# Spacing the router's counts, the token transposes and the weight conversions between the matmuls of a fused attention and expert kernel

## The chip, the cores and the metric

The kernel is one program on one core of a Trainium2 chip. The metric is the device time of one launch in microseconds (us), the median of the runs shown. The kernel before took 1327.54 us, the median of 3 runs (1324.36, 1327.54 and 1327.96). A profile of one execution comes with it.

## The reference, cut to what matters

Three stages follow each other. Block-diagonal attention (8 batches, 8 heads, 576 positions in chunks of 64, head size 64) gives 4608 tokens of 512 numbers. A greedy router then gives every token to one of 8 experts, 576 tokens each, and each expert is a two-layer network. A dense network over all tokens ends it.

```python
logits = x @ w_gate                     # 4608 x 8
for idx in argsort(-logits.flatten()):  # greedy: best pair first
    tok, e = idx // E, idx % E
    if assigned[tok] >= 0 or counts[e] >= cap: continue
    assigned[tok] = e; counts[e] += 1
out[mask_e] = relu(x[mask_e] @ w1[e]) @ w2[e]        # 512 -> 1024 -> 512, per expert
y = max(out @ m1, out @ m2, out @ m3) @ m_out        # 512 -> 768 -> 512, relu inside
```

Matrix products of the experts and of the dense network are run as three products of split numbers (high times high, low weight times high, high weight times low), which is why each weight chunk and each activation has a "hi" and a "lo" tile.

## The kernel before, in words

After attention the kernel knows the logits (tile `L`). The routing is done in 8 rounds, one per expert that fills up. Round 0 runs alone; rounds 1 to 7 are woven between the matmuls of the experts. The order of all instructions is written out by hand: each engine runs its own instructions in the order in which the program issues them.

The weaving works by **places**. The expert loop calls `pump()` after every 6 matmuls of 288 columns, 64 times for each expert (32 times in the first layer, line L777, and 32 in the second, L806), so there are 512 places. `pump()` takes one step of three Python generators: `assign` (the routing), `prepare` (gathering and transposing the tokens of the next expert) and `convert` (rewriting the dense network's weights from 64 bit to 32 bit); at every second place it also calls `pump_loads()`, which splits one landed weight chunk into hi and lo (`split`, L577 on ScalarE, L578 on VectorE) if one is old enough, and issues one new 512 KB load on the SP queue. A `yield n` in a generator means: nothing more of this for n places. If the tokens of the next expert are not all transposed when its turn comes, `pump()` is called without matmuls.

`Router.round` is one round. Rounds 1 to 6 hold 5 search steps that narrow down a threshold. One step is: compare the bids with 32 levels (`ge`, L411, two VectorE instructions); 4 places later a first count on TensorE (L425, 9 matmuls), and VectorE takes from it the products that are wanted (`cs`, L428); one place later a second count (L433, 4 matmuls) and two short VectorE instructions (`fl`, `fb`); one place later a last small matmul (L441) and the new lower bound (`lo`, L443), with which the next step starts at the same place. Around the steps a round has a start (L353 to L399, then 5 places), the selection (L449 to L473), the positions (L478 to L491), the list of token numbers (L497, L504), and the bookkeeping (L509 to L519): in all 50 places. Round 7 has no search step. The chosen expert's 8 weight chunks can be asked for from the selection on (`expert`).

`prepare` gathers the 576 tokens (L597), waits 14 places (10 in round 1), and then transposes one 128-token tile at each place, five in all (`x_tr`: 4 TensorE transposes into one of two PSUM tiles `pxt` at L620, a ScalarE copy `xhi` at L622, a VectorE subtraction `xlo` at L623). It starts no sooner than the first layer of the expert before is through, since `xhi` and `xlo` have one buffer each.

`convert` works through 48 pieces of the dense weights; each is a load of 256 KB (tile `c64`, two buffers, L658), 7 VectorE instructions (L668 to L689), one at each step, and a store (L690). Before round 7 is done it takes a step at every second place, after that at every place. Loads and stores are both on the SP queue. Chunks of the dense weights are asked for only when their pieces are converted.

After expert 7 the dense network runs over 9 blocks of 512 tokens (L857, L880). In block 0 `pump()` and one more step of `convert` follow every 3 matmuls, so that what is left of the conversion runs there at two steps per 3 matmuls. `yload` (L734) brings the block's activations, 1 MB, and `ysplit` (L745, L746) splits them; block 1's load uses the same buffer as block 0's. The first layer's two PSUM tiles `acc` are freed by ScalarE's `ta` (L864) and VectorE's `tb` (L866).

Of the kernel before, what the change touches and what calls it, by code (L numbers as in the profile page):

```python
# [270 lines left out]
class Router:  # L271
# [111 lines left out]
    def round(s, r, PS, e_ready):  # L383
# [18 lines left out]
        for i in range(0 if last else NSTEP):  # L402
            mark("r.step")
            if i:
                lev = W.tile([128, J], F32, name="lev")
                nc.vector.tensor_scalar(lev, s.jw[:, i], lo, None, op0=OP.add)
            else:
                lev = s.lev0
            ge = W.tile([128, G, J], BF, name="ge")
            for a, b in ((0, 18), (18, G)) if r else ((0, 16), (16, 28), (28, G)):  # L410
                nc.vector.tensor_tensor(ge[:, a:b], bid[:, a:b, None].to_broadcast([128, b - a, J]),  # L411
                                        lev[:, None, :].to_broadcast([128, b - a, J]), op=OP.is_ge)
            if r + i == 0:
                s.begin2()
            if r == 0:
                mark("r.cnt")
                pc = PS.tile([128, E], F32, name="rp", tag="rp", bufs=2)
                for c in range(G):
                    nc.tensor.matmul(pc[:J, :], ge[:, c, :], oh[:, c, :], start=c == 0, stop=c == G - 1)  # L419
            else:  # L420
                yield 4
                mark("r.cnt")
                pk = PS.tile([128, 4, E], F32, name="rp", tag="rp", bufs=2)
                for c in range(0, G, 4):
                    nc.tensor.matmul(pk.rearrange("p c e -> p (c e)"), ge[:, c:c + 4].rearrange("p c j -> p (c j)"),  # L425
                                     oh[:, c:c + 4].rearrange("p c e -> p (c e)"), start=c == 0, stop=c == G - 4)
                cs = W.tile([128, 4, E], F16, name="cs")
                nc.vector.tensor_tensor(cs, pk, s.same, op=OP.mult)  # L428
                yield 1
                mark("r.cnt2")  # L430
                pc = PS.tile([128, E], F32, name="rp", tag="rp", bufs=2)
                for c in range(4):
                    nc.tensor.matmul(pc[:J, :], s.lev1, cs[:, c], start=c == 0, stop=c == 3)  # L433
            fl = W.tile([128, 1], F32, name="fl")
            fb = W.tile([128, 1], BF, name="fb")
            nc.vector.tensor_reduce(fl[:J], pc[:J], op=OP.max, axis=AX.X)
            nc.vector.tensor_scalar(fb[:J], fl[:J], CAP - .5, None, op0=OP.is_ge)
            yield 1
            mark("r.lo")
            pn = PS.tile([128, 1], F32, name="rp", tag="rp", bufs=2)  # L440
            nc.tensor.matmul(pn, s.ones[:J, :], fb[:J], start=True, stop=True)  # L441
            nlo = W.tile([128, 1], F32, name="lo", bufs=2)
            nc.vector.scalar_tensor_tensor(nlo, pn, s.ws[:, i:i + 1], lo, op0=OP.mult, op1=OP.add)  # L443
            lo = nlo
# [79 lines left out]
def kernel(ctx, tc, q, k, v, w_gate, w1, w2, m1, m2, m3, m_out, out, mark=lambda n: None):  # L524
# [18 lines left out]
    state = {"issued": 0, "used": 0, "w1": -1, "idx": -1, "pump": 0, "conv": 0}  # L543
# [37 lines left out]
    def pump_loads():  # L581
        for x in inflight:
            x[1] += 1
        if inflight and inflight[0][1] > 6:
            split()
        issue()
# [4 lines left out]
    def gather(r):  # L591
        mark("gather")
        xg = []
        for t in range(5):
            n = 128 if t < 4 else 64
            g = P.tile([128, DM], F32, name="xg", bufs=5)
            nc.gpsimd.indirect_dma_start(out=g[:n], out_offset=None, in_=xd[:, :],  # L597
                                         in_offset=bass.IndirectOffsetOnAxis(ap=rt.idx[r][:n, t:t + 1], axis=0))
            xg.append(g)

        ix, c = rt.idx[r], r // 2 * 9
        if r % 2 == 0:
            nc.gpsimd.tensor_copy(ia[:, c:c + 4], ix[:, 0:4])
            nc.gpsimd.tensor_copy(ia[:64, c + 4:c + 5], ix[:64, 4:5])
        else:
            nc.gpsimd.tensor_copy(ia[64:, c + 4:c + 9], ix[:64, 0:5])
            nc.gpsimd.tensor_copy(ia[:64, c + 5:c + 9], ix[64:, 0:4])
        return xg

    def x_tr(r, xg, t):  # L610
        mark("xg")
        if t == 0:
            XH[r] = [P.tile([128, 4, CAP], F32R, name=n) for n in ("xhi", "xlo")] + [0]
        n = 128 if t < 4 else 64
        if r == 0 and t == 2:
            pt = PS.tile([128, 2, 4, 128], F32, name="acc")[:, 0]
        else:
            pt = PS.tile([128, 4, 128], F32, name="pxt")
        for dc in range(4):
            nc.tensor.transpose(pt[:, dc, :n], xg[t][:n, dc * 128:dc * 128 + 128], rt.ident[:n, :n])  # L620
        hi, lo = (x[:, :, t * 128:t * 128 + n] for x in XH[r][:2])
        nc.scalar.copy(hi, pt[:, :, :n])  # L622
        nc.vector.tensor_tensor(lo, pt[:, :, :n], hi.bitcast(F32), op=OP.subtract)  # L623
        XH[r][2] += 1
# [9 lines left out]
    def prepare():  # L634
        for r in range(1, E):
            while state["idx"] < r:
                yield
            xg = gather(r)
            for _ in range(10 if r == 1 else 14):
                yield  # L640
            while state["w1"] < r - 1:
                yield
            for t in range(5):
                x_tr(r, xg, t)
                yield

    def convert():

# [13 lines left out]
        for i, (_, dst) in enumerate(jobs):  # L662
# [29 lines left out]
            yield  # L692

    assigning, preparing, converting = assign(), prepare(), convert()

    def pump():

        state["pump"] += 1
        next(assigning, None)
        next(preparing, None)  # L700
        if state["idx"] == E - 1:
            next(converting, None)
        elif state["pump"] % 2 and state["pump"] > 16:
            next(converting, None)
        if state["pump"] % 2:
            pump_loads()
# [47 lines left out]
    for r in range(E):  # L754
# [6 lines left out]
        while r and (r not in XH or XH[r][2] < 5):  # L761
            pump()
        hh, hl = (P.tile([128, 8, CAP], F32R, name=n) for n in ("hhi", "hlo"))
        xh, xl, _ = XH[r]
        for f in range(8):
# [4 lines left out]
            for hf in range(2):  # L770
                tk = slice(hf * 288, hf * 288 + 288)
                terms = [(dc, a, x) for dc in range(4) for a, x in ((0, xh), (1, xh), (0, xl))]
                if f == 0:
                    terms.sort(key=lambda t: t[2] is xl)
                for n, (dc, a, x) in enumerate(terms):
                    mark("mm1")
                    nc.tensor.matmul(acc[:, hf, :288], w[a][:, dc, o:o + 128], x[:, dc, tk],  # L777
                                     start=n == 0, stop=n == 11)
                    if n == 5:
                        while r + f == 0 and XH[r][2] < 5:  # L780
                            x_tr(0, xg, XH[r][2])
                        pump()
                if hf == 1:
                    mark("relu")
                    hv = hh[:, f].rearrange("p (a t) -> p a t", a=2)
                    nc.scalar.activation(hv, acc[:, :, :288], AF.Relu)  # L786
                    if f % 2:
                        state["used"] += 1
                    if f == 7:
                        state["w1"] = r  # L790
                pump()
                if hf == 1:
                    mark("relu")
                    nc.vector.scalar_tensor_tensor(hl[:, f].rearrange("p (a t) -> p a t", a=2), acc[:, :, :288],  # L794
                                                   0.0, hv.bitcast(F32), op0=OP.max, op1=OP.subtract)
# [136 lines left out]
```

## Time and profile before

| what | value |
|---|---|
| median of 3 runs | 1327.54 us (1324.36 to 1327.96) |
| time of the profiled execution | 1325.97 us |
| its span, first to last instruction | 1324.2 us |
| TensorE busy over the span | 1258.0 us (95%) |
| VectorE busy over the span | 712.1 us (54%) |
| ScalarE busy over the span | 399.0 us (30%) |
| mean granted TensorE clock | 0.981 of full speed |

The experts run from 229.95 us to 727.01 us of the span and the routing rounds 1 to 7 from there to 568.85 us. How to read it: TensorE's busy time is the sum of its instructions, and its idle time has a releaser, the instruction of another engine that ended last before it went on. VectorE's share is a mean over very different stretches: it is high while the routing runs and low in the dense network.

### The profile page before, as it was taken

How to read it: one execution, taken by the hardware profiler on the slowest of the kernel's cores; microseconds unless marked ns; L12 is line 12 of the kernel's file. 1: busy time of each engine (PE TensorE's matmuls, PEld its weight loads, DVE VectorE, ACT ScalarE, POOL GpSimd, SP SyncE). 2: the span in 40 equal slices, each digit the busy share in tenths (PEclk: the TensorE clock that was granted, in tenths of full speed). 3: DMA queues.
4: the chain of work that ended last, by engine and by line, in shares of the span. 5: the costliest groups of instructions: out<-in, count | busy, mean ns of one | idle time of the engine just before them, and what ended most of it. 6: DMA issues, size and time to landing. Idle time of an engine off the chain costs nothing.

```text
span 1324.2 us, 21335 instructions
## 1 busy us (share of the span) xinstructions
PE 1258.0 (95%) x8605; PEld 1094.5 (83%) x8605; DVE 712.1 (54%) x1572; ACT 399.0 (30%) x709; POOL 103.2 (8%) x172
## 2 busy tenths in 40 slices
PE   6999975998999999999999999999999999999997
PEld 5777753898998899999999888888888888888885
DVE  5777776778888888876857422222222222222221
ACT  5888751323314232233323311111111121212110
POOL 5000001010110101101000000000000000000001
PEclk9999995999999999999999999999999999999999
DMA  8999933262643535456555201010101010100000
GB/s 195 204 214 218 221 99 100 80 195 70 210 139 109 171 97 157 135 160 212 160 175 193 98 9 56 16 49 16 48 16 48 17 48 17 48 24 8 24 9 32
DMA packets 167396, 135.63 MB, mean 102 GB/s; under 512 B 45698, under 2 KB 142466, under 8 KB 167298
## 3 DMA queue, kind: packets, MB, share of 16 engines
q1 hardware_dynamic: 156338, 105.93, 28.9%
q0 software_dynamic: 5824, 18.88, 4.3%
q10 hardware_dynamic: 5136, 9.46, 1.9%
q8 instruction: 68, 1.11, 0.4%
q14 instruction: 30, 0.25, 0.1%
HBM read 99.63 MB, written 34.60 MB: 101 GB/s over the span
## 4 chain that ended last, share of the span: by engine, by line
PE 40%; issue 34%; DVE 7%; POOL 3%; another core or an unknown queue 1%; ACT 1%; DMA 1%; POOLq 0%; SPq 0%; ACTq 0%; DVEq 0%
PE acc L806 14%; PE acc L777 12%; PE acc L857 5%; PE pc L857 3%; DVE chunk L578 3%; PE po L880 2%; POOL out_dram L886 2%; PE rp L504 1%; DVE ge L411 1%; PE pxt L620 1%; DVE hlo L794 1%; PE rp L419 0%; PE rp L433 0%; DMA raw<-in_moe_w_dram 0%
## 5 line engine op out<-in xcount | busy, mean ns | idle before, releaser
L806 PE MATMUL acc<-hhi,chunk 128*128 128x288 f32 x1024 | 213.9, 302 | 0.8 <-DVE hlo L794 0.8
L777 PE MATMUL acc<-xhi,chunk 128*128 128x288 f32 x1024 | 209.3, 304 | 0.7 <-ACT xhi L622 0.7
L806 PEld LDWEIGHTS acc<-hhi,chunk 128*128 128x128 f32 x1024 | 162.8, 188 | 2.3 <-DVE hlo L794 1.2
L777 PEld LDWEIGHTS acc<-xhi,chunk 128*128 128x128 f32 x1024 | 162.7, 191 | 2.4 <-ACT xhi L622 1.1
L866 DVE TENSOR_TENSOR tb<-ta,acc 128x512 f32<-128x512 f32 x54 | 37.1, 687 | 235.0 <-ACT ta L864 235.0
L806 PE MATMUL acc<-hlo,chunk 128*128 128x288 f32 x512 | 150.8, 295 | 0.0
L857 PE MATMUL acc<-yxhi,chunk 128*128 128x512 f32 x480 | 147.8, 389 | 0.0
L777 PE MATMUL acc<-xlo,chunk 128*128 128x288 f32 x512 | 143.9, 297 | 0.0
L857 PE MATMUL acc<-yodd,chunk 128*128 128x512 f32 x576 | 134.5, 389 | 0.0
L857 PEld LDWEIGHTS acc<-yodd,chunk 128*128 128x128 f32 x576 | 108.1, 188 | 22.5
L857 PEld LDWEIGHTS acc<-yxhi,chunk 128*128 128x128 f32 x480 | 90.0, 188 | 18.6
L806 PEld LDWEIGHTS acc<-hlo,chunk 128*128 128x128 f32 x512 | 96.1, 188 | 0.1
L578 DVE TENSOR_TENSOR chunk<-raw,chunk 128x1024 fp32r<-128x1024 f32 x75 | 91.2, 1219 | 8.2 <-ACT chunk L577 8.0
L777 PEld LDWEIGHTS acc<-xlo,chunk 128*128 128x128 f32 x512 | 94.4, 190 | 0.0
L864 ACT COPY ta<-acc 128x512 f32<-128x512 f32 x54 | 31.7, 587 | 205.7 <-PE acc L857 203.7
L857 PE MATMUL acc<-yxlo,chunk 128*128 128x512 f32 x240 | 93.4, 389 | 0.0
L786 ACT ACTIVATE hhi<-acc 128x576 fp32r<-128x576 f32 x64 | 41.8, 652 | 162.0 <-PE acc L777 154.3
L577 ACT CAST chunk<-raw 128x1024 fp32r<-128x1024 f32 x75 | 76.8, 1046 | 34.6 <-DMA raw<-in_moe_w_dram 25.7
L886 POOL DMA_INDIRECT out_dram<-ot,ia x36 | 34.6, 961 | 674.9 <-DVE ot L884 622.2
L880 PE MATMUL po<-chunk,hm 128*128 128x512 f32 x324 | 79.7, 390 | 0.0
L867 DVE TENSOR_TENSOR tb<-tb,pc 128x512 f32<-128x512 f32 x54 | 37.1, 687 | 74.3 <-PE pc L857 74.3
L857 PE MATMUL pc<-yxhi,chunk 128*128 128x512 f32 x240 | 73.9, 389 | 0.0
(193 smaller groups left out, 1908.7 us busy)
## 6 DMA issues: line engine op xcount, KB each, us to landing
raw<-in_moe_w_dram SPq DMA_DIRECT2D x64, 512.0 KB
vb<-in_v_dram SPq DMA_DIRECT2D x144, 64.0 KB
xd<-x SPq DMA_DIRECT2D x36, 256.0 KB
c<-in_moe_w_dram SPq DMA_DIRECT2D x36, 256.0 KB
yd<-ys ACTq DMA_DIRECT2D x32, 288.0 KB
yraw<-yd SPq DMA_DIRECT2D x9, 1024.0 KB
ink<-in_k_dram SPq DMA_DIRECT2D x11, 512.0 KB
inq<-in_q_dram SPq DMA_DIRECT2D x11, 512.0 KB
```

Of the source, the lines that this page charges most:

```text
L411: nc.vector.tensor_tensor(ge[:, a:b], bid[:, a:b, None].to_broadcast([128, b - a, J]), lev[:, None, :].to_broadcast([128, b - a, J]), op=O ...
L577: nc.scalar.copy(hi, raw)
L578: nc.vector.tensor_tensor(lo, raw, hi.bitcast(F32), op=OP.subtract)
L777: nc.tensor.matmul(acc[:, hf, :288], w[a][:, dc, o:o + 128], x[:, dc, tk], start=n == 0, stop=n == 11)
L786: nc.scalar.activation(hv, acc[:, :, :288], AF.Relu)
L806: nc.tensor.matmul(acc[:, hf, :288], w[a][:, f, :], x[:, f, tk], start=n == 0, stop=n == 23)
L857: nc.tensor.matmul(ps, w[a][:, dc, o:o + 128], x[:, dc], start=n == 0, stop=n == 11)
L864: nc.scalar.copy(ta, pab[:, 0])
L866: nc.vector.tensor_tensor(tb, ta, pab[:, 1], op=OP.max)
L867: nc.vector.tensor_tensor(tb, tb, pc, op=OP.max)
L880: nc.tensor.matmul(po, h[:, x, t * 128:t * 128 + 128], w[a][:, f % 2], start=n == 0, stop=n == 17)
L886: st = nc.gpsimd.indirect_dma_start(out=out, out_offset=bass.IndirectOffsetOnAxis(ap=ia[:, 4 * b + t:4 * b + t + 1], axis=0), in_=ot, in_o ...
```

## The change: what it does

Three edits, all in the order of issue; no instruction is added or taken away.

```diff
@@ Router.round, between first and second count
                 nc.vector.tensor_tensor(cs, pk, s.same, op=OP.mult)
-                yield 1
+                yield 1 if r == 1 else 2
                 mark("r.cnt2")
@@ prepare
             for t in range(5):
                 x_tr(r, xg, t)
-                yield
+                for _ in range(1 if r < 3 else 3):
+                    yield
@@ pump
-        elif state["pump"] % 2 and state["pump"] > 16:
+        elif state["pump"] % 2 and state["pump"] > 64:
             next(converting, None)
```

The first edit puts two places instead of one between the first count (with `cs`) and the second count, in all rounds but round 1. The second puts the five token tiles of experts 3 to 7 three places apart. The third lets the conversions start at place 65 instead of place 17.

## Rows read from the trace of the kernel before

**Rows 1.** The page's first part: busy time, share of span, instructions.

```profile
span 1324.2 us, 21335 instructions
PE 1258.0 (95%) x8605; PEld 1094.5 (83%) x8605; DVE 712.1 (54%) x1572; ACT 399.0 (30%) x709; POOL 103.2 (8%) x172
```

**Rows 2.** Windows: length, PE, PEld, DVE, ACT, POOL busy us, clock, DMA, GB/s.

```profile
229.95:568.85 338.90, 323.42 (x2730) 305.21 (x2731) 284.23 (x722) 96.58 (x132) 35.05 (x42) 0.99 0.45 137
568.85:727.01 158.16, 157.76 (x1194) 156.90 (x1193) 115.15 (x247) 53.97 (x74) 5.42 (x8) 1.00 0.57 176
```

**Rows 3.** TensorE's waits, whole run: total us, times, longest.

```profile
PE rp L433 <- DVE cs L428: 10.9, 10, 1.8
...
PE pxt L620 <- DVE xlo L623: 3.5, 4, 1.8
...
PE acc L806 <- DVE hlo L794: 0.8, 2, 0.4
```

**Rows 4.** TensorE in order of time; in brackets idle before and releaser.

```profile
256.72 0.24 PE L433 MATMUL rp<-cs,lev 128*32 128x8 f16 x4 [1.67 <-DVE cs L428]
...
299.64 0.46 PE L620 MATMUL pxt<-ident,xg 64*128 64x64 f32 x4 [1.84 <-DVE xlo L623]
...
317.79 0.24 PE L433 MATMUL rp<-cs,lev 128*32 128x8 f16 x4 [1.78 <-DVE cs L428]
...
454.64 0.24 PE L433 MATMUL rp<-cs,lev 128*32 128x8 f16 x4 [1.53 <-DVE cs L428]
462.21 0.24 PE L433 MATMUL rp<-cs,lev 128*32 128x8 f16 x4 [1.73 <-DVE cs L428]
...
537.40 0.66 PE L620 MATMUL pxt<-ident,xg 128*128 128x128 f32 x4 [0.82 <-DVE xlo L623]
```

**Rows 5.** The chain that ended last, in order of time: start, us, what.

```profile
568.85 25.43 PE acc L777 x192
...
594.73 0.79 PE acc L806 x6
...
743.36 5.44 PE acc L857 x24
```

**Rows 6.** VectorE in order of time, round 1, then round 5.

```profile
253.01 0.29 DVE L668 TENSOR_SCALAR ct<-c 128x256 int32<-128x256 int32 x1
253.21 1.22 DVE L578 TENSOR_TENSOR chunk<-raw,chunk 128x1024 fp32r<-128x1024 f32 x1
...
255.01 0.42 DVE L671 SCALAR_TENSOR_TENSOR ct<-ct,c 128x256 f32<-128x256 f32 x1
255.34 1.22 DVE L578 TENSOR_TENSOR chunk<-raw,chunk 128x1024 fp32r<-128x1024 f32 x1
...
297.55 1.43 DVE L411 TENSOR_TENSOR ge<-bid,lev 128x576 bf16<-128x576 f32 x2
298.89 1.28 DVE L623 TENSOR_TENSOR xlo<-pxt,xhi 128x512 fp32r<-128x512 f32 x2
...
460.83 1.22 DVE L578 TENSOR_TENSOR chunk<-raw,chunk 128x1024 fp32r<-128x1024 f32 x1
461.97 0.18 DVE L428 TENSOR_TENSOR cs<-rp,same 128x32 f16<-128x32 f32 x1
```

**Rows 7.** The window just after the longest wait, columns as in rows 2.

```profile
300.00:305.00 5.00, 5.00 (x36) 4.64 (x35) 3.70 (x10) 2.26 (x3) 0.00 (x0) 0.66 0.53 173
```

**Rows 8.** The SP queue's issues before the dense network, in order of time.

```profile
705.84 1.21 SPq L658 DMA_DIRECT2D c<-in_moe_w_out_dram  x1
...
709.52 0.44 SPq L658 DMA_DIRECT2D c<-in_moe_w_out_dram  x1
...
724.96 0.37 SPq L734 DMA_DIRECT2D yraw<-yd  x1
```

**Rows 9.** VectorE there: its first instruction on each of those two loads.

```profile
709.52 0.29 DVE L668 TENSOR_SCALAR ct<-c 128x256 int32<-128x256 int32 x1 [0.41 <-DMA c<-in_moe_w_out_dram]
...
716.38 0.29 DVE L668 TENSOR_SCALAR ct<-c 128x256 int32<-128x256 int32 x1 [3.05 <-DMA c<-in_moe_w_out_dram]
```

## Prediction

> **What bounds the kernel now.** I read the busy shares first: TensorE is busy for 95% of the span [rows 1]. So a change of order can win back only TensorE's idle time and what the clock loses. I then cut the span into stretches. While experts and routing run together, 229.95 to 568.85 us, TensorE is busy for 323.42 of 338.90 us, so it idles 15.5 us, and VectorE is busy for 284.23 us, 84% [rows 2]. In the rest of the experts' time TensorE idles 0.4 us [rows 2]. The table of waits says who ends that idle time: VectorE in nearly all cases. Ten waits of the second count for `cs` take 10.9 us, four waits of the token transposes for `xlo` 3.5 us, two of the second layer for `hlo` 0.8 us [rows 3]. A wait there does not mean that `cs` is slow (it takes 0.18 us [rows 6]): VectorE works in order, and `cs` stands behind chunk splits of 1.22 us, the comparisons `ge` of 1.43 us a pair, and conversions [rows 6]. TensorE does one place of matmuls, 0.79 us [rows 5], between the first count and the second, and then stands until that queue has come to `cs`.
>
> The longest wait has a second price. After 1.84 us of idling before a transpose [rows 4] the granted clock averages 0.66 from 300 to 305 us [rows 7]. The two levels being 1.0 and 0.5 (2.4 and 1.2 GHz), that is 0.34 x 5 = 1.7 us of full-speed time lost.
>
> **The change part by part.** Nothing is added or removed, and the experts have 512 places before and after. So each place still has its 6 matmuls, and no place without matmuls arises as long as tokens come in time. I counted this from the yields. A round is 50 places, 55 in rounds 2 to 6, and 20 in round 7, which has no search step (so the first edit acts in five rounds, 25 counts). Rounds 1 to 7 then end at places 50, 105, 160, 215, 270, 325 and 345, instead of 50, 100, 150, 200, 250, 300 and 320. The tokens of expert r are needed at place 64r. Expert 2's are transposed at places 119 to 123 of 128, expert 3's end at place 186 of 192, the later ones 15 or more places ahead. The weight splits of experts 2 and 3 begin at places 113 and 169, ahead of 128 and 192. None is late.
>
> *Second place before the second count.* Two of the ten waits are in round 1 (1.67 us [rows 4] and 0.3), 8.9 us in rounds 2 to 6: 1.78, 1.53 and 1.73 [rows 4], and five of about 0.6 to 1.1 that make up the other 3.9. One more place takes 0.79 us off each: 1.0, 0.7 and 0.9 stay of the large ones, and 0.3 of the five, 2.9 us in all. What is issued in the extra place stands behind `cs` in VectorE's queue, so it does not delay that `cs`; it can delay the next step. Rounds 2 to 6 also move against the experts, so other counts meet the bursts of splits (up to five, one at every second place). Counting the splits between `ge` and `cs` step by step, two steps of rounds 2 and 3 that have two now get one or none, so their remaining 1.3 us goes; the first two steps of round 6 get the pattern that round 5's first two have now, 0.7 + 0.9 us. So 3.3 of 8.9 us stay: a gain of 5.6. Bounds: 8.9 if every wait goes, 0 if each comes back elsewhere. I stay with 5.6, as each large wait is about two places long.
>
> *Conversions from place 65.* In round 1 the wait of 1.67 us ends a queue without gaps that holds two conversion instructions, which hold up what follows by 0.20 and 0.33 us (253.01 to 253.21, 255.01 to 255.34 [rows 6]). Without them it is 1.1 us: a gain of 0.5 (bounds 0 and 2.0, all of round 1's waits).
>
> What is put off comes later: 24 steps of places 17 to 63, and since round 7 ends 25 places later, some 12 more. By place 512 about 308 of 337 steps are done, where all are done by place 504 now. The other 29 or so run in dense block 0, two per 3 matmuls, ahead of the first `tb` on VectorE. Behind them: `tb` must free the PSUM tile before the third group of matmuls, at 743.36 us in the old time [rows 5]. The pieces' loads then stand on SP behind block 1's 1 MB `yraw`, issued at 724.96 us when block 0's split has freed its buffer [rows 8]. A load behind such a one came to its first VectorE instruction 6.9 us after issue (709.52 to 716.38), another in 3.7 us (705.84 to 709.52) [rows 8, 9]. So the first late piece starts at about 732, a piece is 2.4 us of VectorE, and a load is issued when the piece two before it is done: pieces at 732, 734.4, 738 and 740.5 us, `tb` done near 742. That leaves about 1.5 us: cost 0, but the cover is thin. If every load takes 6.9 us, `tb` is done near 745 and TensorE stands 2 us; with further 512 KB chunk loads among them, up to 5.
>
> *Transposes at every third place.* For experts 3 to 5, three waits together make 3.5 - 1.84 = 1.7 us, one of 0.82 us [rows 3, 4]; each waits for the `xlo` two tiles back, which now has six places instead of two. They go (bounds 0 and 1.7). Expert 1 keeps its spacing, but the first edit acts on it: the wait of 1.84 us [rows 4] is for an `xlo` that stands behind a step's `ge` pair (297.55, then 298.89 [rows 6]). The step's last matmul now comes one place later, so that `xlo` is issued before the `ge` pair and the wait goes. What is late next is the last tiles' `xlo` at the first matmuls of expert 1 that read it: behind `ge` 1.43, a split 1.22 and its own 1.3 us I get about 0.9 us. Expert 2's transposes now meet a burst of splits: 0.5 us. Sum: 1.7 + 1.84 - 0.9 - 0.5, a gain of 2.1.
>
> *Second layers.* Experts 3 and 4 now begin theirs (places 224 and 288) amid a step and splits, as only expert 2 does now, whose share of the 0.8 us [rows 3] is 0.4: a loss of 0.6 (bounds 0 and 2).
>
> *The clock.* With 1.84 us of idling cut to 0.9 in smaller pieces I let the dip go: a gain of 1.7, at least 0.
>
> Sum: -5.6 - 0.5 - 2.1 + 0.6 - 1.7 = -9.3 us, against the profiled execution's own 1325.97 us: 1316.7. The median of the runs is 1.6 us above it, which gives 1318.2 for a median; I take the middle, 1317.5. By the bounds, the most that can go is 15.5 + 1.7 = 17.2 us.
>
> The Trainium skill speaks against the clock term ("TensorE: Matmul & The Clock Gate", section "A second HAM failure mode: psum-queue depth-cycling"): brief idles of TensorE between groups of matmuls, if frequent, make its clock swing between the two levels. The trace agrees at one place in this stretch only [rows 7]; the waits of 1.67, 1.73 and 1.78 us [rows 4] left the clock at full. By the page the dip need not go, and the sum would be 1.7 us less.
>
> **The rivals.**
>
> *A: the waits only move.* VectorE stays the bound. For: it is 84% busy [rows 2], and in a burst a place brings half a split and half a conversion, about 0.8 us, as much as the place lasts, so what the extra place lets it catch up is gone at the next step. Against: a step now spans 7 places instead of 6 for the same work, and between bursts VectorE has gaps. Then half the `cs` gain and half the transposes' go and the dip stays: 2.8 + 0.5 + 1.0 - 0.6 = 3.7, so 1322 to 1324.
>
> *B: the conversion tail.* The 2 to 5 us at the third group of block 0, as worked out above; all else as forecast: 1320 to 1323. For: three loads in a row behind 1.5 MB. Against: the 1.5 us left. It decides from a mean of about 6 us a load.
>
> The queues bear on this in "DMA: Bandwidth & Descriptors", section "Queues, rings and completion order", of the Trainium skill: on each DMA engine one queue's descriptors are consumed in ring order. The 6.9 us fit that [rows 8, 9]; by it B would be the likelier where chunk loads slip in between.
>
> *C: slower, by the clock.* The 25 counts each leave a small idle (0.7 to 1 us) at closer spacing, and TensorE's clock falls again and again, at 1.7 us a time [rows 7]. From five such dips on nothing is left of the other gains (7.6 us), with eight it is 13.6 - 7.6 = 6 us slower, 1332. For: the one dip in the rows. Against: ten waits now, one dip.
>
> **How the numbers follow.** A measurement of this kernel can tell about 0.3%, 4 us, from no change. The forecast has 0.57, A 0.25, B 0.10, C 0.04, and 0.04 is for gains near the bound or something unseen. Faster: 0.55 of the forecast, 0.08 of A, 0.07 of B, 0.03 of the rest, 0.73. Same: 0.02 + 0.14 + 0.03 + 0.01, 0.20. Slower: 0.03 of A, 0.03 of C, 0.01, 0.07. Range 1311 to 1325: nearly down to the bound, up to the far end of A.
>
> **What would show it.** In the waits by releaser, second count for `cs` at about 4.7 us (round 1 about 1.4); `xlo` before transposes near 0.5 us, and about 1 us before expert 1; no half clock near 300 us. Idle time between 230 and 569 us near 8 us. B would show as a wait on `tb` near 735 us, C as several stretches at half clock, A as 7 us or more of waits for `cs`. Wrong would be a time above 1325.

## The result and the profile after

The changed kernel takes 1337.86 us, the median of 4 runs (1336.88 to 1343.14), against 1325.95 us for the kernel before beside it: a ratio of 1.0102 (of the means), with a 95% interval of 1.0064 to 1.0140. It is about 12 us slower by the medians, where 9 us faster was forecast. In the profiled executions the span went from 1324.2 to 1335.1 us.

The first part of the page after (columns as in [rows 1]) shows no change of work, TensorE's instructions are the same in number:

```profile
span 1335.1 us, 21325 instructions
PE 1260.3 (94%) x8605; PEld 1095.1 (82%) x8605; DVE 712.2 (53%) x1572; ACT 397.8 (30%) x709; POOL 102.1 (8%) x172
```

I cut both spans at the first matmul of the experts' first layer and at the first matmul of the dense network. Attention and round 0 take 1.3 us less in this profile, which the change cannot touch. The experts' time goes from 496.9 to 501.3 us, the dense network from 597.3 to 605.1 us. So more than half of the loss lies in the dense network, which the three edits do not name.

TensorE's waits after, over the whole run, to be held against [rows 3]:

```profile
PE rp L441 <- DVE fb L437: 10.9, 14, 3.0
...
PE acc L858 <- DVE tb L867: 5.5, 1, 5.5
PE rp L433 <- DVE cs L428: 4.3, 6, 1.2
...
PE acc L778 <- DVE hlo L795: 3.4, 2, 2.8
...
PE acc L807 <- DVE hlo L795: 0.9, 2, 0.6
...
PE pxt L620 <- DVE xlo L623: 0.5, 2, 0.4
```

The reader is to see that the waits that the change was to take away did go (`cs` 10.9 to 4.3, `xlo` 3.5 to 0.5), and that three others came up: the step's last matmul (L441) for `fb`, of which 2.1 us lie in round 0 as before and 8.8 us are new; the first layer (L778, before L777) for `hlo`, the low part of that layer's result, with which VectorE frees a PSUM tile `acc`; and dense block 0 for `tb`. The longest of each, in order of time:

```profile
305.37 0.18 PE L441 MATMUL rp<-fb,ones 32*128 32x1 bf16 x1 [2.96 <-DVE fb L437]
...
584.09 0.50 PE L778 MATMUL acc<-xhi,chunk 128*128 128x288 f32 x2 [2.85 <-DVE hlo L795]
...
752.02 1.22 PE L858 MATMUL acc<-yxhi,chunk 128*128 128x512 f32 x2 [5.54 <-DVE tb L867]
```

Behind the first two the clock falls to its lower level for a stretch, and during the third it has already fallen. The windows (columns as in rows 2: PE busy and, third from the end, the granted clock) answer to [rows 7]; 0.83 over 10 us is 1.7 us lost, and 0.76 over the 7.98 us from the end of the third wait is 1.9 us:

```profile
300.00:310.00 10.00, 7.04 (x44) 6.60 (x43) 5.73 (x14) 1.98 (x4) 0.00 (x0) 0.83 0.32 103
580.00:590.00 10.00, 7.16 (x55) 6.59 (x53) 9.83 (x20) 1.58 (x2) 0.00 (x0) 0.83 0.16 47
752.02:760.00 7.98, 7.98 (x27) 6.49 (x28) 6.26 (x11) 2.67 (x4) 0.00 (x0) 0.76 0.17 58
```

Before, there was one such stretch (the first microseconds of the experts, which begin at the lower level in both, left out). The sum nearly closes: among the experts the waits went from 15.5 to 17.9 us and one stretch of 1.7 us was added, 4.1 of the 4.4 us; in the dense network 5.5 us of wait and 1.9 us of clock make 7.4 of the 7.8 us.

**Where `fb` stands.** VectorE before the wait of 2.96 us, in order of time:

```profile
302.98 0.29 DVE L669 TENSOR_SCALAR ct<-c 128x256 int32<-128x256 int32 x1 [2.47 <-DMA c<-in_moe_w_dram]
303.19 1.22 DVE L578 TENSOR_TENSOR chunk<-raw,chunk 128x1024 fp32r<-128x1024 f32 x1
304.32 0.75 DVE L795 SCALAR_TENSOR_TENSOR hlo<-acc,hhi 128x576 fp32r<-128x576 f32 x1
304.99 0.14 DVE L436 TENSOR_REDUCE fl<-rp 32x1 f32<-32x8 f32 x1
305.17 0.15 DVE L437 TENSOR_SCALAR fb<-fl 32x1 bf16<-32x1 f32 x1
```

What the second place issues (a conversion, a split, `hlo`) stands ahead of `fl` and `fb`, and TensorE has only one place of matmuls between the second count and L441. Here the conversion is the very first one, and its load has not come: VectorE stands for 2.47 us.

**Where `hlo` stands.** VectorE before the wait of 2.85 us at 584.09 us, a part of its rows: there is no gap between them.

```profile
577.86 1.22 DVE L578 TENSOR_TENSOR chunk<-raw,chunk 128x1024 fp32r<-128x1024 f32 x1
...
579.33 1.22 DVE L578 TENSOR_TENSOR chunk<-raw,chunk 128x1024 fp32r<-128x1024 f32 x1
580.47 0.30 DVE L481 TENSOR_TENSOR_SCAN base<-rp,z 128x72 f32<-128x72 f32 x1
...
582.46 0.82 DVE L497 TENSOR_TENSOR aoh<-i,md 128x1152 bf16<-128x1152 bf16 x1
583.19 0.75 DVE L795 SCALAR_TENSOR_TENSOR hlo<-acc,hhi 128x576 fp32r<-128x576 f32 x1
```

Two chunk splits and the positions of round 7 (L481 to L497) stand ahead of `hlo`.

**Where `tb` stands.** VectorE around the wait in dense block 0, first the pieces' first instructions and then `tb`:

```profile
728.77 0.29 DVE L669 TENSOR_SCALAR ct<-c 128x256 int32<-128x256 int32 x1
...
736.80 0.29 DVE L669 TENSOR_SCALAR ct<-c 128x256 int32<-128x256 int32 x1 [5.25 <-DMA c<-in_moe_w_out_dram]
...
742.25 0.30 DVE L669 TENSOR_SCALAR ct<-c 128x256 int32<-128x256 int32 x1 [2.66 <-DMA c<-in_moe_w_out_dram]
742.46 1.22 DVE L578 TENSOR_TENSOR chunk<-raw,chunk 128x1024 fp32r<-128x1024 f32 x1
...
745.05 1.22 DVE L578 TENSOR_TENSOR chunk<-raw,chunk 128x1024 fp32r<-128x1024 f32 x1
...
746.98 0.29 DVE L669 TENSOR_SCALAR ct<-c 128x256 int32<-128x256 int32 x1
...
750.55 0.29 DVE L669 TENSOR_SCALAR ct<-c 128x256 int32<-128x256 int32 x1 [0.79 <-DMA c<-in_moe_w_out_dram]
...
751.28 0.69 DVE L867 TENSOR_TENSOR tb<-ta,acc 128x512 f32<-128x512 f32 x1
```

And the SP queue there, with its own waits in that stretch (us in total, times, longest):

```profile
728.09 0.37 SPq L735 DMA_DIRECT2D yraw<-yd  x1
728.55 0.46 SPq L564 DMA_DIRECT2D raw<-mo  x1
729.11 0.42 SPq L691 DMA_DIRECT2D mo<-ct  x1
729.58 0.48 SPq L659 DMA_DIRECT2D c<-in_moe_w_out_dram  x1
731.58 0.32 SPq L691 DMA_DIRECT2D mo<-ct  x1
737.53 0.37 SPq L564 DMA_DIRECT2D raw<-mo  x1
737.96 0.46 SPq L659 DMA_DIRECT2D c<-in_moe_w_out_dram  x1
```

```profile
SPq L564 <- DMA mo<-ct: 5.5, 1, 5.5
```

The chunk load `raw<-mo` reads what the store `mo<-ct` of 731.58 us has just written, so SP holds it until that store has landed, 5.5 us later behind the 1 MB `yraw`, and the next piece's load stands behind it on SP. The piece that waits for 5.25 us had its load issued at 729.58 us, behind `yraw` and a chunk load, and starts 7.2 us later. `tb`, with 24 conversion steps of the block ahead of it in VectorE's order, ends 22 us after the block's start (729.98 us); the third group of matmuls wants it at 16.5 us.

### The profile page after: what moved, and what is told of

Its sections match the earlier page's. It is cut to its first block, busy times and chain, and to the rows that moved or that the text cites. A ratio compares the mean times of both kernels' runs of the same rounds, so it can differ in the third digit from the quotient of the medians.

```text
span 1335.1 us, 21325 instructions
## 1 busy us (share of the span) xinstructions
PE 1260.3 (94%) x8605; PEld 1095.1 (82%) x8605; DVE 712.2 (53%) x1572; ACT 397.8 (30%) x709; POOL 102.1 (8%) x172
## 4 chain that ended last, share of the span: by engine, by line
PE 37%; issue 34%; DVE 8%; POOL 3%; DMA 2%; ACT 1%; another core or an unknown queue 1%; SPq 0%; POOLq 0%; ACTq 0%; DVEq 0%
PE acc L778 12%; PE acc L807 12%; PE acc L858 5%; DVE chunk L578 3%; PE pc L858 2%; PE po L881 2%; POOL out_dram L887 2%; PE rp L504 1%; PE pxt L620 1%; DVE ge L411 1%; DVE hlo L795 1%; DMA c<-in_moe_w_out_dram 1%; DMA c<-in_moe_w_dram 1%; PE rp L419 0%
## 5 line engine op out<-in xcount | busy, mean ns | idle before, releaser
L778 PE MATMUL acc<-xhi,chunk 128*128 128x288 f32 x1024 | 211.2, 305 | 4.2 <-DVE hlo L795 3.4
L778 PEld LDWEIGHTS acc<-xhi,chunk 128*128 128x128 f32 x1024 | 163.7, 192 | 6.4 <-issue 3.0
L778 PE MATMUL acc<-xlo,chunk 128*128 128x288 f32 x512 | 144.7, 298 | 0.0
L778 PEld LDWEIGHTS acc<-xlo,chunk 128*128 128x128 f32 x512 | 94.9, 191 | 0.0
```

## Experiments

The experts' time and the dense network's time are from one profiled execution each, as above; they vary between chips by a microsecond or more, so verdicts are taken from the timed ratios. Differences of ratios are given in percentage points (0.1 points are 1.3 us). Each kernel ran on the same chip as the runs of the kernel before that it is held against. The first four of the experiments and the last two ran on one chip, the four from "late yload" on a second, the four from "no split in the gap" on a third.

| run | ratio (95%) | experts, us | dense, us |
|---|---|---|---|
| the kernel before | 1 | 496.9 | 597.3 |
| the change | 1.0102 (1.0064 to 1.0140) | 501.3 | 605.1 |
| edit 1 alone | 1.0018 (1.0004 to 1.0032) | 500.8 | 597.3 |
| edit 2 alone | 1.0017 (1.0001 to 1.0033) | 498.7 | 597.3 |
| edit 3 alone | 1.0010 (0.9995 to 1.0025) | 497.5 | 597.3 |
| edits 1 and 2 | 1.0025 (1.0011 to 1.0039) | 500.0 | 597.3 |
| the change, late yload | 1.0035 (1.0019 to 1.0052) | 499.0 | 599.3 |
| edit 1, step of six | 0.9968 (0.9957 to 0.9979) | 492.1 | 597.3 |
| edit 1, both gaps | 0.9979 (0.9961 to 0.9996) | 493.5 | 597.3 |
| edit 1, round 7 held | 0.9955 (0.9937 to 0.9973) | 491.4 | 597.3 |
| the same, no split in the gap | 0.9952 (0.9940 to 0.9965) | 489.1 | 597.3 |
| edits 1 and 2, round 7 held | 0.9961 (0.9944 to 0.9978) | 490.3 | 597.3 |
| step of six, edit 2 | 0.9969 (0.9954 to 0.9984) | 494.6 | 597.3 |
| both gaps, edit 2, round 7 held | 0.9932 (0.9910 to 0.9953) | 487.5 | 597.3 |
| before, round 7 in the first layer | 1.0026 (1.0015 to 1.0036) | 499.8 | 597.3 |
| before, tail alone | 1.0028 (1.0016 to 1.0040) | 492.9 | 602.8 |

**The three edits apart.** Each is the hunk shown with the change.

Edit 1:

> Edit 1 alone: two places between the two counts, transposes at every place, conversions from place 17. Theory M (the wait moves one count down): VectorE's fl and fb, which the last small matmul of the step (L441) waits for, now stand behind what the extra place issues (a chunk split of 1.22 us, hlo, a conversion). Waits of the second count for cs fall from 10.9 to about 4 us, waits of L441 for fb come up to about 9 us among the experts, as in the changed kernel; and the first layer of expert 5 waits about 3 us for hlo, with a stretch of half clock, since round 7 now lies in it. By place count only 5 of 336 conversion steps are left for dense block 0, so no wait on tb there. In sum 3 to 6 us slower than before. Rival T (all of the loss is the tail of conversions in dense block 0): then this kernel is 0 to 3 us faster than before.

Measured: 0.18% slower. `cs` 4.4 us, `fb` 5.6 us among the experts, `hlo` in the first layer 2.8 us with half clock behind it, no wait on `tb`. Theory M's waits are there, `fb` smaller than expected, and rival T fell: this is not faster.

Edit 2:

> Edit 2 alone: transposes of experts 3 to 7 three places apart. Theory M and rival T agree here: waits of the transposes for xlo fall by the 1.7 us of experts 3 to 5, the wait of 1.84 us of expert 1 and its half clock stay, nothing else changes: 1 to 2 us faster, which may not be told from no change. If xlo's VectorE time shifted into the search steps cost more than it wins, waits for cs or fb rise above 11 us and it is slower.

Measured: 0.17% slower, a miss. `xlo` fell to 1.8 us as expected, but `cs` rose from 10.9 to 13.1 us in 13 waits, and there are two stretches of half clock instead of one. The edit explains only half of the rise. Two of the new waits, 0.79 and 0.47 us, lie at 292 and 302 us in round 2, where the order of issue is still that of before (the first transpose that is moved comes at 406 us). Around those moved transposes, in round 4, `cs` waits for 2.5 us where it waited for 1.4: there the `xlo` subtractions that were together now lie in the search steps.

Edit 3:

> Edit 3 alone: conversions from place 65. By place count 16 of 336 conversion steps are left for dense block 0 (29 in the changed kernel), so two loads stand behind the 1 MB yraw load instead of four. Theory T' (the tail costs by its loads): the first tb in block 0 comes at about 11 us after the block's start, before the third group's 16.3 us, so no wait or under 1 us there; round 1's cs wait falls by 0.5 us; time within 1 us of before. Rival (any step left over costs the wait): a wait on tb of 3 us or more and half clock after it, 4 to 8 us slower.

Measured: 0.10% slower, not told from no change; no wait on `tb` with 16 steps left over, and the longest `cs` wait of round 1 falls from 1.67 to 1.14 us, both as expected.

Edits 1 and 2 without 3:

> Edits 1 and 2 without edit 3 (conversions from place 17): 5 steps left for dense block 0. Theory: the wait of 5.5 us on tb and the half clock behind it (3 us) vanish, the waits on fb (about 9 us) and on hlo in expert 5 (2.9 us, with 1.7 us of clock) stay: 8 us faster than the changed kernel, 2 to 5 us slower than before. Rival (the tail is only where a VectorE delay from the rounds shows up): a wait on tb stays, and the time stays within 3 us of the changed kernel's 1338.

Measured: 0.25% slower, 0.77 points less than the change, 10 us. The wait on `tb` is gone, the others stay (`fb` 6.7 us, `hlo` in the first layer 2.8 us). The dense network makes 7.8 of the 10 us; in the rounds the longest wait for `fb`, 2.96 us, falls to 0.85. So in the changed kernel the tail needs edits 1 and 3 together: 16 steps are left by edit 3, 5 by edit 1, 29 by both.

**What makes the tail.** The changed kernel with this:

```diff
                 ysplit(0, yr)
-                yr = yload(1)
...
             layer1(b, f)
+            if f == 1 and b == 0:
+                yr = yload(1)
```

> The changed kernel, with block 1's 1 MB load yraw issued after the second group of dense block 0 instead of before the last conversions, so that the loads of the late conversion pieces do not stand behind it. Theory D (the tail's wait is load time): VectorE's idle time for those loads, 5.3 + 2.7 + 0.8 us in the changed kernel, falls below 4 us, the wait of 5.5 us on tb and the half clock behind it go, 7 to 9 us faster than the changed kernel, about 1328. Rival W (the tail's wait is VectorE's own work, 24 conversion steps and two or three splits ahead of the first tb, or the chunk loads): the wait on tb stays above 3 us and the time above 1333.

Measured: 0.35% slower than before, so 0.67 points or 8.9 us better than the change. By the profiles 5.8 us of this are the dense network's (605.1 to 599.3). The experts' 2.3 us cannot be the edit's, as the order is the same up to expert 7's second layer. The wait on `tb` and SP's wait for the store, in the stretch of the block:

```profile
PE acc L857 <- DVE tb L866: 1.5, 1, 1.5
```

```profile
SPq L564 <- DMA mo<-ct: 1.5, 1, 1.5
```

Theory D holds for most of it: loads and the store's landing behind 1 MB. VectorE's idle time for the pieces' loads is 4.7 us, a little more than expected, and 1.5 us of wait remain.

**The new wait for `fb`.** Edit 1 with three places ahead of the first count:

```diff
-                yield 4
+                yield 4 if r == 1 else 3
```

> Edit 1 alone, with three places instead of four between the comparisons and the first count in rounds 2 to 6, so that a step stays at six places and every round ends where it did before. Theory M (the wait moves one count down, and the later rounds cost a wait for hlo in expert 5): waits of L441 for fb stay at 5 us or more among the experts; the wait of 2.8 us for hlo in expert 5's first layer and its half clock go, since round 7 lies in the second layer of expert 4 again. From the start of the experts to the dense network about 497 us, where edit 1 alone took 500.8 and the kernel before 496.9. Rival N (the fb waits come from the shift of the rounds against the chunk splits, not from the place itself): fb waits below 2 us and 490 to 493 us.

Measured: 0.32% faster, 492.1 us, `fb` 1.5 us. Theory M missed here and rival N met its numbers: with the same two gaps after the first count, but each round at its old place against the bursts of splits, the wait for `fb` is mostly absent. The long `hlo` wait went, as both said. In its place come small waits of the first count for `ge`, 1.7 us in six.

The same step with a second place also before the last matmul, in a round of 55 places:

```diff
-            yield 1
+            yield 2 if r > 1 else 1
             mark("r.lo")
```

> Edit 1 alone, and in rounds 2 to 6 also two places before the last small matmul, three instead of four before the first count: 55 places a round as with edit 1. Theory M: fb waits fall from 5.6 to 2 us or less, cs waits rise at most to about 6 us as one place is taken ahead of the first count, the hlo wait of 2.8 us with its half clock stays since round 7 lies where edit 1 puts it: 497 to 499 us of experts' time against 500.8 for edit 1 alone. Rival V (VectorE is the bound and any wait taken here comes back elsewhere): all waits among the experts together stay at 13 to 16 us and the experts' time at 500 us or more.

Measured: 0.21% faster. No wait for `fb` at all, `cs` 3.9 us, `hlo` in the first layer 3.4 us with its half clock. The experts' time fell further than expected, in part because edit 1 alone ran on a chip where `cs` waits longer (next experiment); V fell.

**Round 7.** Edit 1 with this in `assign`:

```diff
         for r in range(1, E):
+            while r == E - 1 and state["pump"] < 352:
+                yield
```

> Edit 1 alone, with round 7 held back to place 352, the second layer of expert 5 (edit 1 lets it run from place 326, in the first layer). Theory H: the wait of 2.8 us for hlo in expert 5's first layer and the stretch of half clock after it are round 7's VectorE work meeting hlo and chunk splits there; both go, the experts' time falls by 4 to 4.5 us from 500.8 to about 496.5. Some 18 conversion steps are left for the dense block 0, no wait on tb (edit 3 alone left 16). Rival: the wait is of the conversions at every place and stays, or comes back at a wait on tb; the time does not fall.

Measured: 0.45% faster. The long `hlo` wait and the half clock are gone, and no stretch of half clock is left among the experts. The fall is twice what was expected, 9.4 us in the profiles; waits for `cs` fell too (4.4 to 2.0 us), though the order of issue is the same until place 326. Two ScalarE rows, of edit 1 and of this kernel, show why:

```profile
345.87 0.64 ACT L813 COPY ys<-acc 128x576 f32<-128x576 f32 x1 [8.86 <-remote]
```

```profile
343.97 0.64 ACT L815 COPY ys<-acc 128x576 f32<-128x576 f32 x1 [6.91 <-PE acc L808]
```

In edit 1's profile the same copy starts 1.9 us late for a reason that the profile does not name, and with it the splits behind it on ScalarE, VectorE's halves of them, and `cs`. This goes with the chip. In the eight profiles from the two other chips no copy of this kind starts more than 0.7 us after the last matmul of its block; five of the six from this chip, and those of the two kernels before and after, have copies 1.2 to 2.7 us after it. The late yload run has the changed kernel's order up to expert 7 and none of these late copies, and its `cs` waits are 1.9 us instead of 4.3. So about 2.4 us of the fall are not round 7's, and the run with round 7 moved alone, further down, puts a figure on round 7.

The same kernel, and no split from `cs` to `fb` (the first line of the cut stands behind `cs`, the second behind `fb`; `free` lets through the splits that a matmul needs at once):

```diff
+                s.hold = r > 1
...
+            s.hold = False
...
-        if inflight and inflight[0][1] > 6:
+        if inflight and inflight[0][1] > 6 and not (rt.hold and len(chunks) >= 8 and state["free"]):
```

> Edit 1 with round 7 held to place 352 (as the run before, 1318 us, experts' time 491.4), and no chunk split issued from cs until fl and fb are issued, in rounds 2 to 6; a split that is due comes up to two places later. Theory M (what is issued in the extra place stands ahead of fl and fb, and chunk splits are most of it): the six waits of L441 for fb, 4.4 us, fall below 1.5 us, cs waits rise by less than 2 us, the experts' time is 489 to 490 us. Rival V (VectorE's queue as a whole is behind, and what is taken from before fb comes back before cs or in the transposes): waits for fb, cs and xlo together stay at about 8.8 us and the time does not move.

Measured: 0.48% faster, 489.1 us. The waits for `fb` before (edit 1 with round 7 held) and with the split kept out:

```profile
PE rp L441 <- DVE fb L437: 4.4, 6, 1.3
```

```profile
PE rp L444 <- DVE fb L439: 0.2, 1, 0.2
```

Theory M is shown for the size of `fb`: without splits in the extra place it is gone. The splits alone do not make it, though: the traces have 14 of them between `cs` and `fl` in rounds 2 to 6 with edit 1, and 12 in the step of six, where `fb` is waited for 1.5 us. How far VectorE is behind when they come must differ, and no run takes that apart. Of the 4.2 us, 3.0 came back at `cs` (3.9) and `xlo` (3.5), so V is right about most of the balance; the timed ratio does not tell it from the run without.

**Both causes taken away.** Edits 1 and 2 with round 7 held, conversions from place 17:

> Edits 1 and 2 with round 7 held to place 352 and conversions from place 17: the changed kernel with its two causes of loss taken away. Theory: no wait on tb in dense block 0 (18 conversion steps left), no long wait for hlo in expert 5, transposes' waits for xlo fall from 2.4 to under 1 us: 1316 to 1318 us, 20 us less than the changed kernel. Rival (spacing the transposes moves xlo into the search steps and costs waits there, as edit 2 alone had 2.2 us more waits for cs): waits for cs and fb rise by 2 us or more and the time stays at 1318 to 1320.

Measured: 0.39% faster, 1318.1 us; `xlo` 0.4 us, but `fb` 5.4 and `cs` 2.5. It lies between theory and rival: spacing the transposes is worth nothing here, but 1.41 points, about 19 us, lie between this and the changed kernel; some 2.4 of them go with the late copies.

> The step of six places (three before the first count, two between the counts; 1319.4 us, experts' time 492.1) with edit 2. Theory: the transposes' waits for xlo fall by 1.6 us, the one of expert 1 with its half clock stays; 490 to 491 us of experts' time. Rival as for the held kernel: the xlo that now lie in the search steps cost as much, 492 us or more.

(The edit is the step of six with edit 2.) Measured: 0.31% faster, as without edit 2. `xlo` fell to 1.8 us as expected, but this profile has a stretch of 6.8 us at half clock from 543 us, behind two waits of 0.34 and 0.25 us, hence 494.6 us; a miss.

> Three, two and two places in a step of rounds 2 to 6 (experts' time 493.5 with a wait of 2.8 us for hlo in expert 5 and its half clock), edit 2, and round 7 held to place 352. Theory: the hlo wait and its half clock go (4.5 us), fb waits stay at 0: 488 to 489 us of experts' time and the fastest of all, about 1315 us. Rival: with 55 places a round and three places ahead of the first count the waits come at cs instead, more than 5 us of them, 491 us or more.

(The edits are both gaps, edit 2 and the held round 7.) Measured: 0.68% faster, 1313.8 us, the fastest of all, and faster than both kernels. `fb` 0.2 us, `cs` 4.3 of which 2.0 in round 1, `hlo` 1.5, no stretch of half clock among the experts once they have started.

**Each cause alone, added to the kernel before.**

```diff
         for r in range(1, E):
+            while r == E - 1 and state["pump"] < 326:
+                yield
```

> The kernel before with one thing added: round 7 held to place 326, so that it lies in the first layer of expert 5, where the changed kernel has it (before: from place 301, in the second layer of expert 4). Theory H: a wait of 2 to 3 us for hlo in expert 5's first layer and a stretch of half clock behind it (1.7 us lost) come up, 3 to 5 us slower than before. Rival (the wait needs the crowded rounds of the changed kernel ahead of it, or was a disturbed ScalarE): no such wait, time within 1.5 us of before.

Measured: 0.26% slower, 3.4 us, with the waits of theory H:

```profile
574.52 0.53 PE L779 MATMUL acc<-xhi,chunk 128*128 128x288 f32 x2 [1.08 <-DVE hlo L796]
...
583.46 0.50 PE L779 MATMUL acc<-xhi,chunk 128*128 128x288 f32 x2 [1.82 <-DVE hlo L796]
```

The clock stayed at full there. A stretch at half came from 459 us, but that is ahead of place 326, where nothing was changed yet.

```diff
-        elif state["pump"] % 2 and state["pump"] > 16:
+        elif state["pump"] % 2 and state["pump"] > 88:
```

> The kernel before with conversions from place 89 instead of 17 and nothing else, so that 28 conversion steps are left for dense block 0 (29 in the changed kernel, 16 with edit 3 alone). Theory D: a wait of 4 to 6 us on tb at the third group of block 0 with half clock behind it, the time from the start of the dense network to the end 604 to 606 us instead of 597.3, 7 to 9 us slower than before, less some 0.5 us that the rounds win. Rival (the tail needs the later rounds too): no wait on tb, time within 1 us of before.

Measured: 0.28% slower, 3.7 us; the dense network takes 602.8 us. Theory D's wait is there, smaller than expected (3.3 us and one stretch of half clock), without edit 1. The row of the wait:

```profile
739.91 0.50 PE L857 MATMUL acc<-yxhi,chunk 128*128 128x512 f32 x1 [3.33 <-DVE tb L866]
```

In this profile the waits among the experts are 3 us less than before, where 0.5 us were expected of the postponed conversions; edit 3 alone had not shown this.

So 28 steps are enough to make a tail, whichever edit leaves them over; its size differs, 5.5 us of dense time here and 7.8 in the changed kernel.

## Why the prediction was wrong, step by step

Three costs were put at nothing: 8.8 us of waits for `fb`, 7.8 us of tail in the dense network, and 2.8 us of wait for `hlo` in expert 5. The clock, which was to give back 1.7 us, took 1.7 us more among the experts. Together that is about 23 us; forecast and result are 21 us apart, as the other terms came out a little better than forecast.

- *The count of places* held: round ends, 29 steps left over, tokens and splits in time, no place without matmuls.
- *Second place before the second count.* The sum of this term came out, 4.7 us of waits for `cs` forecast and 4.3 measured, but partly by luck: 2.4 of the 4.3 us, in rounds 3 and 4, go with the late copies of the chip (the late yload run has 1.9), and the 1.6 us forecast for round 6 did not come at `cs`. The step that failed is "it can delay the next step". What the extra place issues delays the same step, at `fb`, and 8.8 us of waits came up there, 2.7 of them in round 6's first two steps. The prediction followed the queue to `cs` and did not follow it on to the next matmul that waits on VectorE. Rival A had this in general (the waits only move), but with the wait still at `cs`, and without the rest.
- *Conversions from place 65.* In round 1 right: 1.67 us became 1.14. But the first conversion now falls into a search step of round 2, with its load not yet there (2.47 us of VectorE), which makes the longest wait for `fb` (2.96 us; the same step waits 0.83 us with edit 1 alone) and the stretch of half clock near 305 us.
- *The tail* was priced at 0, rival B at 2 to 5 us. Measured: 5.5 us of wait and 1.9 us of clock. The pieces were to start 5, 7.4, 11 and 13.5 us after the block's start, with `tb` done near 15; they start at 6.8, 12.3, 17.0 and 20.6, and `tb` is done at 22. The first load took 7.2 us. Then the step failed that says "a load is issued when the piece two before it is done": SP also held a chunk load for 5.5 us until the store that it reads had landed behind `yraw`, and the next piece's load stood behind that. Two chunk splits of 1.22 us stand ahead of the third piece, and a piece takes 2.8 us of VectorE, not 2.4. Taking `yraw` out of the way took 5.8 us off the dense network.
- *Transposes.* `xlo` was forecast at 0.5 us and is 0.5, and the 0.9 us expected before expert 1 did not come. The gain did not stay, though: by itself the edit made `cs` about 1 us worse in round 4, and with round 7 held it was worth nothing.
- *Second layers.* A loss of 0.6 was forecast at `hlo`; it was 0.1. What was not seen at all is expert 5's *first* layer. I moved round 7's end from place 320 to 345 and followed its effect on conversions and tokens, but did not look at what else VectorE does at places 326 to 345: an `hlo` at every fourth place, splits, and then conversions. That is 2.8 of the 3.4 us (the other 0.5 are in expert 3 and stay when round 7 is held) and a stretch of half clock; moved alone it costs 0.26%.
- *The clock* was forecast to give back 1.7 us, and lost 3.6 more: one stretch before, three after, each at one of the three longest waits. So rival C, many small waits, was not what happened. The rule of the Trainium skill that was weighed there ("TensorE: Matmul & The Clock Gate", section "A second HAM failure mode: psum-queue depth-cycling") says that frequent brief idles between matmul groups make the clock swing. The traces do not show that the number of waits decides it: edits 1 and 2 together have 23 waits among the experts and one stretch, the step of six with edit 2 has 17 and two.

The tail (7.8 us in the profile, 5.8 of them because `yraw` stands ahead) and round 7 (0.26% alone) are shown to cost their parts. For `fb` the splits in the extra place are shown to be needed (4.4 us with them, 0.2 without), but 3.0 us of that came back at other waits. Undoing round 7's move gave more, 0.47 to 0.64 points. Of the 0.63 for edit 1 and the 0.64 for edits 1 and 2, about 0.18 (an estimate from the 2.4 us) are the late copies, since these pairs lie on different chips. The 0.47 (both gaps, where edit 2 was added too) is free of them, and it includes the stretch of half clock that the move alone did not bring. What makes ScalarE's copies late stays open.

## What to carry to other kernels

When work is spaced out in a hand-written order, follow the in-order queue past the wait that is to go, up to the next instruction that anyone waits for, and count what the new place issues ahead of that one. When a stage ends later, list every other stage that starts from its end (here the conversions' rate and the place of the next round), find where their work lands, and look at what is on the same engine there. In this kernel a load that reads what was just stored holds everything behind it on SP until the store has landed, and a large transfer ahead of the store makes that longer: 5.5 us behind the 1 MB load, 1.5 us with it moved away.

## What the runs showed of the hardware

TensorE's clock level does not follow the length of one wait. In the run with round 7 moved alone, waits of 1.39 and 1.74 us for `cs` came with a stretch at half clock, and the `hlo` wait of 1.82 us with none (windows as above):

```profile
454.00:464.00 10.00, 8.26 (x60) 7.74 (x59) 8.37 (x18) 2.26 (x4) 0.00 (x0) 0.83 0.53 146
582.00:592.00 10.00, 8.54 (x82) 8.36 (x83) 8.96 (x18) 1.90 (x3) 0.00 (x0) 1.00 0.34 93
```

The wait before expert 1's transposes is another case: 1.84 us in the kernel before, with a stretch at half behind it [rows 4, 7], and 1.83 us in the run with edit 2 alone, with none:

```profile
298.00:308.00 10.00, 9.46 (x86) 8.73 (x87) 9.47 (x21) 4.26 (x6) 0.00 (x0) 1.00 0.33 104
```

So a term for the clock is uncertain by at least one stretch, 1.7 us, each way.
